# Second layer's down product: high and low weight halves side by side as one moving operand of 512 columns

## The chip, the core and the metric

The kernel runs on one core of one Trainium2 chip. The metric is the device time of one execution, in microseconds (us). Before the change three runs took 3819.11, 3821.22 and 3822.73 us; their median is 3821.22 us.

The engines are named as in the profile: PE is TensorE's matmul, PEld its loading of the stationary operand, DVE is VectorE, ACT is ScalarE, POOL is GpSimd, SP is SyncE. The SBUF holds operands, the PSUM (banks of 512 float32 columns on 128 partitions) takes what PE writes.

## The reference, cut to what matters

Three steps follow each other: a convolution along the sequence by FFT, a layer of eight experts with one expert per row, and a dense layer with a squared ReLU. The change is in the last of them.

```python
def _moe2_ref(x, w_in, w_out):          # x: 24576 x 256
    h = np.maximum(x @ w_in, 0.0)       # w_in: 256 x 2048
    return (h * h @ w_out).astype(np.float32)   # w_out: 2048 x 256

def reference(**kwargs):
    attn_out = _attn_ref(**attn_kwargs)          # irfft(rfft(x) * filt), 8 x 3072 x 256
    x = attn_out.reshape(B * S, D)
    x = _moe_ref(x=x, **moe_kwargs)              # w1: 8 x 256 x 1024, w2: 8 x 1024 x 256
    return _moe2_ref(x=x, **moe2_kwargs)
```

The inputs w_in and w_out come as float64; the kernel's matmuls take float32 operands in the rounded form fp32r, so every factor is split into a high part and a low part, and a product is high by high, plus high by low, plus low by high.

## The kernel before, in words

The kernel runs its stages one behind the other on one core: the FFT stage, the expert layer ("layer 1" below, functions up and down, lines 793 to 831), and the dense layer ("layer 2", functions split_t, up2, split_h and down2, lines 853 to 943). Layer 1 multiplies with moving operands of 512 columns (some tiles 256), layer 2 with 256. While layer 1 runs, DVE decodes the float64 weights of layer 2 into high and low parts (decode_all) that stay in SBUF: `woh` and `wol` are the halves of w_out.

Layer 2 takes the 24576 rows in 48 tiles of 512 rows (index t) and the 2048 hidden columns in 8 units of 256 (index u): 384 steps (t, u). The up product up2 forms four 128 x 256 blocks from seven products (prod, line 879); each is three matmuls of 256 columns, 21 in all. They collect in three PSUM banks: V (pool psH, two buffers), G (psX) and P (psH2). ACT and DVE bring them out: ACT copies s1 (L888), p5 (L890), u2 (L895) and C[2] (L903); DVE adds C[0] (L893), C[3] (L899) and C[1] (L900). DVE squares the ReLU into q (L905), split_h rounds q into hh on ACT (L912) and takes the rest hl on DVE (L914).

The down product down2 multiplies slices of hh and hl (stationary, 128 x 128) with rows of woh and wol (moving, 256 columns): 24 matmuls per step, three for each of eight combinations of row block and hidden half. They add up over the 8 units in two PSUM banks, each with the 256 output columns of two row blocks. Tiles with even t use the banks of pool psY, those with odd t the banks of psY2 (py_tiles). After the last unit ACT copies each bank to SBUF (L933) and POOL scatters each row block to the output with an indirect DMA (L936).

The order on each engine is the order in which the code issues. The loop at lines 1025 to 1041 handles three units at a time, in four parts: in pass n, up2 of unit n, split_h of unit n - 1 (ACT's hh in part 1, DVE's hl in part 2, counting from 0) and down2 of unit n - 2. In each part up2 comes first, then split_h, then the piece of down2. So the last down2 of tile t (u = 7) is issued in the pass in which up2 works on unit u = 1 of tile t + 1. Below this pass is called the closing pass of tile t. In it, as in every pass, part 1 of up2 ends with the second product into V and its copy u2; part 2 has the second product into G, the third into V, and the adds L899 (which reads V) and L900 (which reads G); part 3 starts with the fourth product into the same V.

Of the kernel before, what the change touches and what calls it, by code (L numbers as in the profile page):

```python
# [12 lines left out]
F32 = mybir.dt.float32  # L13
F32R = mybir.dt.float32r
# [3 lines left out]
ALU = mybir.AluOpType  # L18
# [4 lines left out]
B, S, D = 8, 3072, 256  # L23
NT = B * S
E, F1 = 8, 1024
F2 = 2048
# [4 lines left out]
TT = 512  # L31
# [71 lines left out]
def spectral_moe_kernel(ctx: ExitStack, tc: tile.TileContext, x, filt_r, filt_i, w_gate, w_og, w1, w2,  # L103
                        w_in, w_out, c_ma, c_mi, c_mb, c_mb2, c_sg, c_cum, out):
    nc = tc.nc
# [6 lines left out]
    outv = dram_disjoint_views(out, NT // 128)  # L112
# [49 lines left out]
    pl = {"xsm": ctx.enter_context(tc.tile_pool(name="xsm", bufs=2, side="right"))}  # L162
# [455 lines left out]
    w2nd, lpool = [], []  # L618
    dcs = ctx.enter_context(ExitStack())

    def decode(pool, src, parts, val=None):


        v = nc.vector
        raw = pool.tile([128, ND, 2], I32, name="raw")
        nc.sync.dma_start(out=raw, in_=src)
        yield
        H, L = raw[:, :, 1], raw[:, :, 0]
        ea = pool.tile([128, ND], I32, name="ea")
        eb = pool.tile([128, ND], I32, name="eb")  # L630
        v.tensor_scalar(ea, H, 20, 0x7FF, op0=ALU.logical_shift_right, op1=ALU.bitwise_and)
        v.tensor_scalar(eb, ea, 896, 0, op0=ALU.subtract, op1=ALU.max)
        v.tensor_scalar(ea, eb, 255, None, op0=ALU.min)
        v.tensor_scalar(eb, ea, 23, None, op0=ALU.logical_shift_left)
        yield
        v.tensor_scalar(ea, H, -2147483648, None, op0=ALU.bitwise_and)
        v.tensor_tensor(eb, ea, eb, ALU.bitwise_or)
        yield
        v.tensor_scalar(ea, H, 0xFFFFF, 3, op0=ALU.bitwise_and, op1=ALU.logical_shift_left)
        mb_ = pool.tile([128, ND], I32, name="mb_")  # L640
        v.tensor_scalar(mb_, ea, 0x3F800000, None, op0=ALU.bitwise_or)
        P = eb.bitcast(F32)
        a = pool.tile([128, ND], F32, name="a")
        v.tensor_tensor(a, mb_.bitcast(F32), P, ALU.mult)
        yield
        v.tensor_scalar(ea, L, 1, None, op0=ALU.logical_shift_right)
        lf = pool.tile([128, ND], F32, name="lf")
        v.tensor_scalar(lf, ea, 2.0 ** -51, None, op0=ALU.mult)
        v.tensor_tensor(lf, lf, P, ALU.mult)
        yield  # L650
        if val is not None:
            v.tensor_tensor(val, a, lf, ALU.add)
        for at, hi, lo in parts:
            v.tensor_tensor(hi, a[:, at], lf[:, at], ALU.add)
            v.tensor_tensor(a[:, at], a[:, at], hi.bitcast(F32), ALU.subtract)
            v.tensor_tensor(lo, a[:, at], lf[:, at], ALU.add)
        yield

    def decode_all():
        wres = ctx.enter_context(tc.tile_pool(name="wres", bufs=1))  # L660


        wsh, wsl = (wres.tile([128, F2 // 256, 7, 128], F32R, name=n) for n in ("wsh", "wsl"))
        woh, wol = (wres.tile([128, F2 // 128, D], F32R, name=n) for n in ("woh", "wol"))
        w2nd.extend((wsh, wsl, woh, wol))
        lpool.append(ctx.enter_context(tc.tile_pool(name="rp2", bufs=2)))
        pool = dcs.enter_context(tc.tile_pool(name="dcp", bufs=1))
        first, second = slice(0, 128), slice(128, 256)
        for u in range(F2 // 256):
            a0, a1 = (pool.tile([128, ND], F32, name=f"val{c}") for c in range(2))  # L670
            for c, val in enumerate((a0, a1)):
                yield from decode(pool, w_in32[c * 128:(c + 1) * 128, 2 * u * ND:2 * (u + 1) * ND]
                                  .rearrange("p (n two) -> p n two", two=2),
                                  [(at, wsh[:, u, i], wsl[:, u, i])
                                   for at, i in (((first, 0),), ((first, 1), (second, 2)))[c]], val)
            sc = pool.tile([128, 4, 128], F32, name="sc")
            v.tensor_tensor(sc[:, 0], a0[:, second], a1[:, second], ALU.add)
            v.tensor_tensor(sc[:, 1], sc[:, 0], a0[:, first], ALU.subtract)
            v.tensor_tensor(sc[:, 2], a0[:, first], a0[:, second], ALU.subtract)
            v.tensor_tensor(sc[:, 3], a1[:, first], sc[:, 1], ALU.subtract)  # L680
            yield
            nc.scalar.copy(wsh[:, u, 3:7], sc)
            v.tensor_tensor(wsl[:, u, 3:7], sc, wsh[:, u, 3:7].bitcast(F32), ALU.subtract)
            yield
        for f in range(F2 // 128):
            yield from decode(pool, w_out32[f * 128:(f + 1) * 128].rearrange("p (d two) -> p d two", two=2),
                              [(slice(0, D), woh[:, f, :], wol[:, f, :])])


    psm = ctx.enter_context(ExitStack())  # L690
# [18 lines left out]
    def py_tiles(t):  # L709
        return [pl["psY2" if t % 2 and "psY2" in pl else "psY"].tile([128, TT], F32, name=f"py{h}") for h in range(2)]  # L710
# [6 lines left out]
    slot, k = [], 0  # L717
# [120 lines left out]
    NU = F2 // 256  # L838
    R, X2, H2, Z = {}, {}, {}, {}
# [78 lines left out]
    def down2(t, u):  # L918

        hh, hl = H2[t, u]  # L920
        woh, wol = w2nd[2:4]
        if u == 0:
            Z[t] = [p.rearrange("p (c d) -> p c d", c=2) for p in py_tiles(t)]
        for m in range(24):
            k, i, c, n = m // 12, m // 6 % 2, m // 3 % 2, m % 3
            x, w = ((hh, woh), (hl, woh), (hh, wol))[n]
            nc.tensor.matmul(Z[t][k][:, c, :], x[:, 2 * i + k, c * 128:(c + 1) * 128], w[:, 2 * u + i, :],  # L927
                             start=u == 0 and m in (0, 12), stop=u == NU - 1 and m in (11, 23), skip_group_check=True)
            if u == NU - 1 and m in (11, 23):
                if k == 0:  # L930
                    Z[t].append(pl["oup"].tile([128, 4, D], F32, name="ou"))
                ou = Z[t][2]
                nc.scalar.copy(ou[:, 2 * k:2 * k + 2, :], Z[t][k])  # L933
                io = X2[t][2]
                for c in range(2 * k, 2 * k + 2):
                    nc.gpsimd.indirect_dma_start(out=outv[4 * t + c], out_offset=bass.IndirectOffsetOnAxis(ap=io[:, c:c + 1], axis=0),  # L936
                                                 in_=ou[:, c, :], in_offset=None)
            if m in (2, 8, 17):
                yield
        del H2[t, u]  # L940
        if u == NU - 1:
            del X2[t], Z[t]
        yield
# [59 lines left out]
    def steps_m():  # L1003
        for n in range(len(jobs) + LAG1):
            if n < len(jobs):
                t, f = jobs[n]
                up(t, f)
                step_1(t, f)
            if n >= LAG1:
                down(*jobs[n - LAG1])  # L1010
            yield
        for _ in dec[0]:
            pass
        dcs.close()
        used = nc.values_load(usedi[0:1, 0:1], min_val=0, max_val=NTILE_T)
        with tc.If(used > NTILE_T - NX):
            for t in range(NMAIN, NTILE1):
                extra(t)
        m1.close()
        xgs.close()  # L1020
        open_m2()
        st = split_t(0)
        for _ in st:
            pass
        for n in range(len(units2) + 2):
            g = up2(*units2[n]) if n < len(units2) else iter(())
            t, u = units2[min(n, len(units2) - 1)]
            d = down2(*units2[n - 2]) if n >= 2 else iter(())
            for part in range(4):
                next(g, None)  # L1030
                if part == 0 and 0 < n <= len(units2):
                    sh = split_h(*units2[n - 1])
                if part in (1, 2) and n:
                    next(sh, None)
                next(d, None)
            if u == 2 and t + 2 < NTILE2:
                load_t(t + 2)
            if u == 3 and t + 1 < NTILE2:
                st = split_t(t + 1)
            next(st, None)  # L1040
            yield
# [43 lines left out]
    m = steps_m()  # L1085
# [4 lines left out]
    for i, k in enumerate(order):  # L1090
# [3 lines left out]
        n = done["a"]  # L1094
# [24 lines left out]
    tables()  # L1119
    open_left()  # L1120
    dec.append(decode_all())
    for _ in m:
        pass
# [33 lines left out]
```

## Time and profile before

| what | value |
|---|---|
| median of three runs | 3821.22 us |
| profiled execution, its time | 3831.18 us |
| profiled execution, its span (first to last instruction) | 3829.5 us |
| mean granted clock of PE | 0.994 |
| PE busy | 3762.7 us, 98% of the span |
| DVE busy | 2767.0 us, 72% |
| ACT busy | 1973.5 us, 52% |
| POOL busy | 608.2 us, 16% |
| layer 2's matmuls of down2 (L927) | 3 x 3072 |
| layer 2's stretch | from about 1800 us to the end |

The busy time of PE is the sum over pipelined matmuls whose ends are modelled, so a matmul's length in a row (0.28 us for 256 columns) is longer than the step from its start to the next start. The step is what a matmul costs in a dense stream, and it is read from the first column of the timeline.

### The profile page before, as it was taken

What the parts mean: (1) busy time and instruction counts of PE and PEld (TensorE: products, weight loads), DVE (VectorE), ACT (ScalarE), POOL (GpSimd) and SP (SyncE); (2) the same over time, 40 slices, a digit from 0 to 9 for tenths busy, and PEclk for the clock granted to TensorE, in tenths of its full rate; (3) what the DMA queues carried; (4) which work ended last, traced back from release to release, by engine and by line L of the source; (5) the groups of instructions that cost most, each with busy time, mean ns of one, the idle gap of its engine ahead of it and who ended that gap; (6) DMA issues with size and microseconds to landing.
All of it is one profiled execution on the core that took longest, in us unless ns stands there. A gap on an engine that the chain in (4) does not pass through costs nothing.

```text
span 3829.5 us, 73425 instructions
## 1 busy us (share of the span) xinstructions
PE 3762.7 (98%) x27256; PEld 3512.9 (92%) x27256; DVE 2767.0 (72%) x5038; ACT 1973.5 (52%) x3909; POOL 608.2 (16%) x641
## 2 busy tenths in 40 slices
PE   8999999999999999999999999999999999999998
PEld 7888877788888888888999999999999999999998
DVE  6678685688888866655777777777777777777776
ACT  6466463354545545544555555555555555555554
POOL 3477575000000000000001100100110010011001
PEclk9999999999999999999999999999999999999999
DMA  6333322455555545543010010001001000100100
GB/s 194 100 117 113 105 86 91 142 158 165 170 163 173 178 150 161 164 148 114 23 29 23 29 29 23 29 23 29 23 29 29 23 29 23 29 23 29 29 18 18
DMA packets 262750, 309.30 MB, mean 81 GB/s; under 512 B 75153, under 2 KB 206194, under 8 KB 262386
## 3 DMA queue, kind: packets, MB, share of 16 engines
q1 hardware_dynamic: 242928, 252.39, 21.8%
q0 software_dynamic: 18432, 51.93, 3.8%
q8 instruction: 215, 3.52, 0.4%
q14 instruction: 149, 1.22, 0.1%
q10 hardware_dynamic: 1026, 0.23, 0.0%
HBM read 224.01 MB, written 80.45 MB: 80 GB/s over the span
## 4 chain that ended last, share of the span: by engine, by line
PE 37%; issue 14%; POOL 2%; DVE 0%; ACT 0%; POOLq 0%; DVEq 0%; ACTq 0%
PE py L927 20%; PE ph L881 13%; PE px L881 5%; POOL out_dram L936 2%; DVE tc L867 0%; DVE bl L871 0%; DVE hl L914 0%; DVE bl L861 0%; ACT bh L869 0%; POOLq L1152 0%; DVE C L899 0%; ACT ou L933 0%; ACT bh L860 0%; ACT u L895 0%; DVE C L900 0%
## 5 line engine op out<-in xcount | busy, mean ns | idle before, releaser
L927 PE MATMUL py<-woh,hh 128*128 128x256 f32 x3072 | 857.2, 279 | 0.0
L927 PE MATMUL py<-woh,hl 128*128 128x256 f32 x3072 | 852.8, 278 | 0.4 <-DVE hl L914 0.4
L927 PE MATMUL py<-wol,hh 128*128 128x256 f32 x3072 | 852.9, 278 | 0.0
L936 POOL DMA_INDIRECT out_dram<-ou,ix x192 | 214.0, 1115 | 2935.7 <-ACT ou L933 2891.8
L927 PEld LDWEIGHTS py<-woh,hl 128*128 128x128 f32 x3072 | 579.9, 189 | 0.9 <-DVE hl L914 0.8
L927 PEld LDWEIGHTS py<-woh,hh 128*128 128x128 f32 x3072 | 579.9, 189 | 0.0
L927 PEld LDWEIGHTS py<-wol,hh 128*128 128x128 f32 x3072 | 576.3, 188 | 0.0
L806 ACT ACTIVATE hh<-ph 128x512 fp32r<-128x512 f32 (+1 forms) x472 | 251.8, 533 | 586.3 <-PE ph L802 559.3
L881 PE MATMUL ph<-bh,wsh 128*128 128x256 f32 x1920 | 541.5, 282 | 5.6 <-ACT bh L860 4.4
L881 PE MATMUL ph<-bh,wsl 128*128 128x256 f32 x1920 | 539.2, 281 | 0.0
L881 PE MATMUL ph<-bl,wsh 128*128 128x256 f32 x1920 | 539.0, 281 | 0.0
L905 DVE SCALAR_TENSOR_TENSOR q<-C 128x1024 f32<-128x1024 f32 x384 | 468.3, 1220 | 2.3 <-ACT C L903 2.2
L808 DVE SCALAR_TENSOR_TENSOR hl<-ph,hh 128x512 fp32r<-128x512 f32 (+1 forms) x472 | 286.8, 608 | 253.4 <-ACT hh L806 248.5
L914 DVE TENSOR_TENSOR hl<-q,hh 128x1024 fp32r<-128x1024 f32 x384 | 467.1, 1217 | 1.1 <-ACT hh L912 1.1
L899 DVE TENSOR_TENSOR C<-ph,p 128x256 f32<-128x256 f32 x384 | 163.5, 426 | 417.1 <-ACT hh L912 412.8
L903 ACT COPY C<-ph 128x256 f32<-128x256 f32 x384 | 143.0, 372 | 519.7 <-PE ph L881 518.2
L912 ACT CAST hh<-q 128x1024 fp32r<-128x1024 f32 x384 | 403.1, 1050 | 1.3 <-DVE q L905 1.3
L881 PEld LDWEIGHTS ph<-bh,wsh 128*128 128x128 f32 x1920 | 363.0, 189 | 6.9 <-issue 4.6
L881 PEld LDWEIGHTS ph<-bl,wsh 128*128 128x128 f32 x1920 | 361.6, 188 | 0.0
L881 PEld LDWEIGHTS ph<-bh,wsl 128*128 128x128 f32 x1920 | 361.5, 188 | 0.0
L819 PE MATMUL py<-hh,wh 128*128 128x512 f32 (+1 forms) x944 | 348.4, 369 | 0.0
L802 PE MATMUL ph<-xh,wh 128*128 128x512 f32 (+1 forms) x944 | 340.3, 360 | 0.0
(261 smaller groups left out, 8184.2 us busy)
## 6 DMA issues: line engine op xcount, KB each, us to landing
r<-in_moe_w_dram SPq DMA_DIRECT2D x448, 256.0 KB
xt<-in_x_dram SPq DMA_DIRECT2D x48, 512.0 KB
r<-ytd SPq DMA_DIRECT2D x48, 512.0 KB
xg<-srt SPq DMA_DIRECT2D x41, 544.0 KB
ytd<-yt SPq DMA_DIRECT2D x41, 512.0 KB
xg<-srt SPq DMA_DIRECT2D x18, 272.0 KB
ytd<-yt SPq DMA_DIRECT2D x18, 256.0 KB
raw<-in_moe_w_in_dram SPq DMA_DIRECT2D x16, 256.0 KB
```

Of the source, the lines that this page charges most:

```text
L802: nc.tensor.matmul(ps, a[:, c, f2 * 128:(f2 + 1) * 128], b[:, c, 0:w], start=n == 0, stop=n == 5)
L806: nc.scalar.activation(hh, ps, AF.Relu)
L808: nc.vector.scalar_tensor_tensor(hl, ps, 0.0, hh.bitcast(F32), op0=ALU.max, op1=ALU.subtract)
L819: nc.tensor.matmul(Y[t][h], a[:, f % 2, h * 128:(h + 1) * 128], b, start=f == 0 and i == 0, stop=f == NF - 1 and i == 2)
L881: nc.tensor.matmul(ps, x[:, u, a], y[:, b], start=start and n == 0, stop=n == 2, skip_group_check=True)
L899: nc.vector.tensor_tensor(C[:, 3], V, p5, ALU.add)
L903: nc.scalar.copy(C[:, 2], V)
L905: nc.vector.scalar_tensor_tensor(q, C, 0.0, C, op0=ALU.max, op1=ALU.mult)
L912: nc.scalar.copy(hh, q)
L914: nc.vector.tensor_tensor(hl, q, hh.bitcast(F32), ALU.subtract)
L927: nc.tensor.matmul(Z[t][k][:, c, :], x[:, 2 * i + k, c * 128:(c + 1) * 128], w[:, 2 * u + i, :], start=u == 0 and m in (0, 12), stop=u == ...
L936: nc.gpsimd.indirect_dma_start(out=outv[4 * t + c], out_offset=bass.IndirectOffsetOnAxis(ap=io[:, c:c + 1], axis=0), in_=ou[:, c, :], in_o ...
```

## The change

The two halves of w_out are stored side by side in one tile `wo`, so that for each row of 128 hidden values the 256 high columns and the 256 low columns are 512 neighbouring columns. In down2 a slice of hh now multiplies all 512 columns in one matmul, and a slice of hl the 256 high columns. The left half of the bank then collects high by high and low by high, the right half high by low. So a step has 16 matmuls, eight of 512 and eight of 256 columns, where it had 24 of 256. Each row block needs a whole bank: four banks per tile, two of psY and two of psY2, for every t. At the end of a tile, for each of the four row blocks b, ACT copies the left half to SBUF (now 256 columns), DVE adds the right half to it, and POOL's indirect DMA waits for DVE.

```diff
-        woh, wol = (wres.tile([128, F2 // 128, D], F32R, name=n) for n in ("woh", "wol"))
-        w2nd.extend((wsh, wsl, woh, wol))
+        wo = wres.tile([128, F2 // 128, 2, D], F32R, name="wo")
+        w2nd.extend((wsh, wsl, wo))
...
         if u == 0:
-            Z[t] = [p.rearrange("p (c d) -> p c d", c=2) for p in py_tiles(t)]
-        for m in range(24):
-            k, i, c, n = m // 12, m // 6 % 2, m // 3 % 2, m % 3
-            x, w = ((hh, woh), (hl, woh), (hh, wol))[n]
-            nc.tensor.matmul(Z[t][k][:, c, :], x[:, 2 * i + k, c * 128:(c + 1) * 128], w[:, 2 * u + i, :],
-                             start=u == 0 and m in (0, 12), stop=u == NU - 1 and m in (11, 23), skip_group_check=True)
-            if u == NU - 1 and m in (11, 23):
-                if k == 0:
+            Z[t] = [pl[n].tile([128, TT], F32, name=f"py{h}") for n in ("psY", "psY2") for h in range(2)]
+        for m in range(16):
+            b, i, n = m // 8 * 2 + m // 2 % 2, m // 4 % 2, m % 2
+            w = D if n else 2 * D
+            at = 2 * i + b // 2, slice(b % 2 * 128, b % 2 * 128 + 128)
+            nc.tensor.matmul(Z[t][b][:, 0:w], (hl if n else hh)[:, at[0], at[1]],
+                             wo[:, 2 * u + i].rearrange("p s d -> p (s d)")[:, 0:w],
+                             start=u == 0 and i == 0 and n == 0, stop=u == NU - 1 and i == 1, skip_group_check=True)
+            if u == NU - 1 and i == 1 and n == 1:
+                if b == 0:
                     Z[t].append(pl["oup"].tile([128, 4, D], F32, name="ou"))
...
-                nc.scalar.copy(ou[:, 2 * k:2 * k + 2, :], Z[t][k])
...
+                nc.scalar.copy(ou[:, b, :], Z[t][b][:, 0:D])
+                nc.vector.tensor_tensor(ou[:, b, :], Z[t][b][:, D:2 * D], ou[:, b, :], ALU.add)
+                nc.gpsimd.indirect_dma_start(out=outv[4 * t + b], out_offset=bass.IndirectOffsetOnAxis(ap=X2[t][2][:, b:b + 1], axis=0),
+                                             in_=ou[:, b, :], in_offset=None)
-            if m in (2, 8, 17):
+            if m in (1, 5, 11):
                 yield
```

The points at which down2 hands over to up2 keep the same share of columns in each part: 3, 6, 9 and 6 matmuls of 256 columns before, 2, 4, 6 and 4 matmuls (half of them of 512) now.

DVE's order in the closing pass of one tile, before: the adds of up2, hl, the square q, and then the next pass.

```order
L893 TENSOR_TENSOR C<-ph,s_27598 128x256
L899 TENSOR_TENSOR C<-ph,p_27599 128x256
L900 TENSOR_TENSOR C<-px,u_27600 128x256
L914 TENSOR_TENSOR hl_27622<-q,hh_27621 128x1024
L905 SCALAR_TENSOR_TENSOR q<-C 128x1024
```

The same pass on DVE now (L936 is the new add of a bank's right half; each new name of py is one of the four banks):

```order
L893 TENSOR_TENSOR C<-ph,s_26983 128x256
L936 TENSOR_TENSOR ou<-py_26573,ou 128x256
L899 TENSOR_TENSOR C<-ph,p_26984 128x256
L900 TENSOR_TENSOR C<-px,u_26985 128x256
L914 TENSOR_TENSOR hl_27006<-q,hh_27005 128x1024
L936 TENSOR_TENSOR ou<-py_26574,ou 128x256
L905 SCALAR_TENSOR_TENSOR q<-C 128x1024
L936 TENSOR_TENSOR ou<-py_26575,ou 128x256
L936 TENSOR_TENSOR ou<-py_26576,ou 128x256
```

Four adds are new; the first stands between L893 and L899, the second between hl and q, the other two behind q.

ACT's order in the closing pass now (before, one L933 of 512 columns stood behind L912 and one behind L903):

```order
L888 COPY s_26983<-ph 128x256
L890 COPY p_26984<-px 128x256
L895 COPY u_26985<-ph 128x256
L912 CAST hh_27005<-q 128x1024
L935 COPY ou<-py_26573 128x256
L935 COPY ou<-py_26574 128x256
L903 COPY C<-ph 128x256
L935 COPY ou<-py_26575 128x256
L935 COPY ou<-py_26576 128x256
```

The copy of the first bank stands directly behind the rounding of hh; DVE's first add reads what this copy writes.

## Rows read from the trace of the kernel before

**Rows 1.** The page: the span, and PE's line of busy time.

```profile
span 3829.5 us, 73425 instructions
PE 3762.7 (98%) x27256; PEld 3512.9 (92%) x27256; DVE 2767.0 (72%) x5038; ACT 1973.5 (52%) x3909; POOL 608.2 (16%) x641
```

**Rows 2.** Busy time by stretch: layer 2's. Columns: window, length, then engines in us.

```profile
core 0: us, PE busy (x) PEld busy (x) DVE busy (x) ACT busy (x) POOL busy (x), PEclk, DMA share, GB/s
1850.00:3790.00 1940.00, 1940.00 (x16678) 1939.69 (x16676) 1429.86 (x2222) 1009.66 (x2132) 210.21 (x188) 1.00 0.09 26
```

**Rows 3.** Timeline of PE, layer 2, one pass. Columns: start, length, engine, line, operation.

```profile
2524.76 0.28 PE L881 MATMUL ph<-bh,wsh 128*128 128x256 f32 x1
...
2525.79 0.28 PE L881 MATMUL ph<-bh,wsh 128*128 128x256 f32 x1
...
2527.21 0.28 PE L881 MATMUL px<-bh,wsh 128*128 128x256 f32 x1
...
2527.56 0.28 PE L881 MATMUL ph<-bh,wsh 128*128 128x256 f32 x1
...
2528.93 0.28 PE L881 MATMUL ph<-bh,wsh 128*128 128x256 f32 x1
...
2529.99 0.28 PE L881 MATMUL ph<-bh,wsh 128*128 128x256 f32 x1
```

**Rows 4.** Timeline of PE in layer 1, where 512 and 256 columns mix.

```profile
1201.01 0.39 PE L802 MATMUL ph<-xh,wh 128*128 128x512 f32 x1
...
1203.05 0.28 PE L802 MATMUL ph<-xh,wh 128*128 128x256 f32 x1
1203.16 0.28 PE L802 MATMUL ph<-xl,wh 128*128 128x256 f32 x1
...
1203.76 0.40 PE L819 MATMUL py<-hh,wh 128*128 128x512 f32 x1
...
1205.15 0.28 PE L802 MATMUL ph<-xh,wh 128*128 128x256 f32 x1
...
1207.60 0.28 PE L802 MATMUL ph<-xh,wh 128*128 128x256 f32 x1
...
1210.00 0.28 PE L819 MATMUL py<-hh,wl 128*128 128x256 f32 x1
```

**Rows 5.** Timeline of ACT in one closing pass.

```profile
2521.53 0.37 ACT L895 COPY u<-ph 128x256 f32<-128x256 f32 x1 [0.68 <-PE ph L881]
2521.79 1.05 ACT L912 CAST hh<-q 128x1024 fp32r<-128x1024 f32 x1
```

**Rows 6.** Timeline of DVE in the same closing pass.

```profile
2521.18 0.42 DVE L893 TENSOR_TENSOR C<-ph,s 128x256 f32<-128x256 f32 x1 [0.45 <-PE ph L881]
2522.94 0.43 DVE L899 TENSOR_TENSOR C<-ph,p 128x256 f32<-128x256 f32 x1 [1.33 <-ACT hh L912]
2523.28 0.41 DVE L900 TENSOR_TENSOR C<-px,u 128x256 f32<-128x256 f32 x1
2523.61 1.22 DVE L914 TENSOR_TENSOR hl<-q,hh 128x1024 fp32r<-128x1024 f32 x1
```

**Rows 7.** Timeline of PE in the same closing pass: the end of part 1, the start of part 3.

```profile
2521.86 0.28 PE L927 MATMUL py<-wol,hh 128*128 128x256 f32 x1
...
2523.69 0.28 PE L881 MATMUL ph<-bh,wsh 128*128 128x256 f32 x1
```

**Rows 8.** Timeline of layer 2's first passes: ACT, DVE and PE, each waiting for another.

```profile
1799.88 1.04 ACT L869 CAST bh<-tc 128x1024 fp32r<-128x1024 f32 x1 [2.02 <-DVE tc L867]
...
1800.95 1.23 DVE L871 TENSOR_TENSOR bl<-tc,bh 128x1024 fp32r<-128x1024 f32 x1 [1.11 <-ACT bh L869]
...
1811.13 0.42 DVE L899 TENSOR_TENSOR C<-ph,p 128x256 f32<-128x256 f32 x1 [1.31 <-PE ph L881]
...
1811.61 0.39 PE L881 MATMUL ph<-bh,wsh 128*128 128x256 f32 x1 [0.59 <-DVE C L899]
...
1811.84 0.28 PE L881 MATMUL ph<-bl,wsh 128*128 128x256 f32 x1
```

More of the change, by code (lines that the diff above doesn't have):

```diff
@@ L686, in decode_all @@
             yield from decode(pool, w_out32[f * 128:(f + 1) * 128].rearrange("p (d two) -> p d two", two=2),
-                              [(slice(0, D), woh[:, f, :], wol[:, f, :])])
+                              [(slice(0, D), wo[:, f, 0], wo[:, f, 1])])
     psm = ctx.enter_context(ExitStack())
@@ L920, in down2 @@
         hh, hl = H2[t, u]
-        woh, wol = w2nd[2:4]
+        wo = w2nd[2]
         if u == 0:
-            Z[t] = [p.rearrange("p (c d) -> p c d", c=2) for p in py_tiles(t)]
-        for m in range(24):
-            k, i, c, n = m // 12, m // 6 % 2, m // 3 % 2, m % 3
-            x, w = ((hh, woh), (hl, woh), (hh, wol))[n]
-            nc.tensor.matmul(Z[t][k][:, c, :], x[:, 2 * i + k, c * 128:(c + 1) * 128], w[:, 2 * u + i, :],
-                             start=u == 0 and m in (0, 12), stop=u == NU - 1 and m in (11, 23), skip_group_check=True)
-            if u == NU - 1 and m in (11, 23):
-                if k == 0:
-                    Z[t].append(pl["oup"].tile([128, 4, D], F32, name="ou"))
-                ou = Z[t][2]
-                nc.scalar.copy(ou[:, 2 * k:2 * k + 2, :], Z[t][k])
[L934 to L937, printed above, removed]
-            if m in (2, 8, 17):
+            Z[t] = [pl[n].tile([128, TT], F32, name=f"py{h}") for n in ("psY", "psY2") for h in range(2)]
[8 more added lines that the diff above has]
+                if b == 0:
+                    Z[t].append(pl["oup"].tile([128, 4, D], F32, name="ou"))
+                ou = Z[t][4]
+                nc.scalar.copy(ou[:, b, :], Z[t][b][:, 0:D])
[3 more added lines that the diff above has]
+            if m in (1, 5, 11):
                 yield
```

## The prediction

> **What bounds the kernel now.** I read the page's head first: PE is busy 98% of the span [rows 1], so the question is only whether PE's stream gets shorter or gets new holes. Then the busy times by stretch: in the 1940 us of layer 2 between 1850 and 3790 us PE is never idle, at a granted clock of 1.00 (the 2.4 GHz level), DVE is busy 1429.86 us (74%) and ACT 1009.66 us (52%) [rows 2]. 16678 matmuls of 256 columns in 1940 us are 116.3 ns from start to start. DVE and ACT have time to spare on average; what counts is whether one of their instructions that PE waits for comes later than PE does. For that I read the timeline.
>
> **What a matmul of layer 2 costs.** One pass, from the first product into V to the next, takes 2529.99 - 2524.76 = 5.23 us for 45 matmuls [rows 3], 116.2 ns each. Within it the step is not even: 12 matmuls from 2527.56 to 2528.93 take 114.2 ns each, 12 from 2525.79 to 2527.21 take 118.3 ns [rows 3]. In layer 1, 9 matmuls of 512 columns from 1201.01 to 1203.05 take 226.7 ns each [rows 4]: twice 113.3, so a column costs the same there as in layer 2's quick stretches, and a wide matmul as such saves little. Where layer 1 alternates six matmuls of 256 and six of 512, the wide ones take (1205.15 - 1203.76)/6 = 231.7 ns and the narrow ones (1203.76 - 1203.05)/6 = 118.3 ns, but the first narrow one behind a wide one takes 0.11 us (1203.05 to 1203.16) [rows 4].
>
> **Removed: eight matmuls and eight weight loads per step.** Three matmuls of 256 columns become one of 512 and one of 256: the columns, 768, stay the same, and what can go is only the part of a matmul's cost that doesn't grow with its columns. Before, three cost 3 x 116.2 = 348.6 ns. The pair is not in the trace of before in this order. Lower end: 226.7 + 114.2 = 340.9 ns, a gain of 7.7 ns. Upper end: 231.7 + 118.3 = 350.0 ns, a loss of 1.4 ns. The nearest rows are those of the mixed stretch, since the new stream mixes too, and in it every narrow matmul stands right behind a wide one: 231.7 + 114.2 = 345.9 ns, a gain of 2.7 ns. There are 8 x 384 = 3072 such threes: -8.3 us, with ends -23.7 and +4.3 us. All of it is on the path, as PE has no idle time here.
>
> **Added: four adds on DVE and two more copies on ACT per tile.** By busy time this is nothing: an add like L893 takes 0.42 us [rows 6], four of them 1.7 us in a tile of 8 x 5.23 = 41.8 us, in which DVE has 26% idle. But the first add stands in DVE's queue between L893 and L899, and it waits for ACT's copy, which stands behind the rounding of hh. Followed through the closing pass in the trace:
>
> - PE finishes the first bank's last matmul at the end of part 1, about 2521.86 + 0.28 = 2522.14 [rows 7]; the columns of part 1 are unchanged.
> - ACT starts hh at 2521.79 for 1.05 us, to 2522.84 [rows 5]. The copy behind it is long released. Neighbours on ACT overlap by 0.11 us (L895 ends at 2521.90, L912 starts at 2521.79 [rows 5]), so the copy starts at 2522.73 and, as 256 columns like L895, takes 0.37 us: 2523.10.
> - DVE has been idle since 2521.60 and waits. An instruction released by ACT starts 0.03 us after ACT's end (1799.88 + 1.04 = 1800.92, then 1800.95 [rows 8]): the add starts at 2523.13.
> - L899 follows it at the distance that L900 has from L899, 0.34 us [rows 6]: at 2523.47 instead of 2522.94, ending at 2523.90 instead of 2523.37.
> - Part 3's first matmul writes the V bank that L899 reads and must wait for it. Layer 2's second pass shows this wait and its price: L899 ends at 1811.13 + 0.42 = 1811.55, the matmul starts at 1811.61, and the next one 0.23 us later, 0.11 us more than the usual step [rows 8]. So here: start at 2523.96 instead of 2523.69 [rows 7], and 0.11 us more behind it: 0.38 us.
>
> Tiles 0 to 46 have such a pass (the last tile's closing pass has no up2): 47 x 0.38 = +17.9 us. Bounds: if the copy could start when the bank is ready, the add would be done before L899 was due, and the price is 0; if each hand-over takes 0.1 us more than in the rows (two of them), 0.58 us, 27.3 us.
>
> Does PE win it back? No: it is the engine without slack, and the three-unit pipeline only moves on. Is something else late next? With all times moved as above, hl starts at 2523.47 + 0.67 = 2524.14 [rows 6] and ends at 2525.36; its first use is the eighth matmul of the next pass, before seven steps of 116.2 ns after 2524.76 [rows 3], at 2525.57, now 0.38 us later, so it is in time by 0.6 us. The second add ends near 2525.7, q near 2526.8, the last two adds near 2527.5. The next pass's L899 was due near 2528.2 and is due 0.4 us later now, so the delay ends there.
>
> **Four banks for every tile instead of two in turn.** The next tile's first down2 writes the same four banks in the next pass. The first bank is free at 2523.5 and written after 2525.4; the last is free near 2527.5 and written in part 2 of the next pass, where layer 2's part 2 starts at 2527.21 [rows 3] and six matmuls of up2 and four of down2 stand before it, so after 2528.6. Over a microsecond is left: no cost. The decode of w_out writes the same number of elements with the same instructions, under layer 1: no cost.
>
> **Sum.** -8.3 + 17.9 = +9.6 us on the profiled execution's 3831.18 us. That execution is 10 us (0.26%) above the median of the three runs, most of layer 2 being the same work in both, so I add the difference to the median: 3821.2 + 9.6 = 3831 us, 0.25% slower. Measurement of this kernel tells about 0.2%, 7.6 us, from no change.
>
> **Rivals.**
>
> (a) Instructions bind, not columns. In layer 1's run of narrow matmuls each takes exactly (1210.00 - 1207.60)/20 = 120.0 ns [rows 4], 6 ns more than in the quick stretches, as if each load and matmul cost a fixed time to hand out. If layer 2's 116.2 ns are a mix of such a bound and of columns at 113.3 ns per 256, then a pass with 37 instead of 45 pairs is bound by columns alone, up2's 21 matmuls too: 45 x (116.2 - 113.3) = 130 ns less per pass, x 384 = -50 us; with the wait above -32 us, 3789 us. For it: the even 120.0. Against it: six wide matmuls behind such a run still cost 231.7 rather than 226.7 ns each, though their pairs have time to be handed out, and layer 2 has quick stretches of twelve narrow ones. By half of it the time is 3821 - 25 + 18 = 3814 us.
>
> The Trainium skill, page "TensorE: Matmul & The Clock Gate", section "Wait — 56ns, not 53.3ns?", says that where hardware decoding is off the sequencer spends about 62 ns on each matmul and becomes the bound once a matmul's work in the array is shorter. The run at 120.0 ns for a load and a matmul fits twice 60; layer 2's 114.2 ns does not. By that rule 37 pairs would take 37 x 120 = 4.44 us, below the 5.1 us of columns, which is rival (a) at its full size.
>
> (b) The wait doesn't show, because the gain in part 0 to 2 or a quicker copy lets L899 come in time: -8.3 us alone, 3813 us. For it: PE's slack to L899 is only missed by 0.3 us. Against it: hh's rounding is 1.05 us long and stands ahead of the copy in the order.
>
> (c) The wait is dearer, or spreads: the adds two to four push q and the next L893 far enough that the next pass waits as well, at the same place and price: 2 x 17.9 - 8.3 = +27.5 us, 3849 us. It decides if DVE's chain in the closing pass is 0.7 us longer than I made it.
>
> **Chances.** Forecast 0.58; (a) 0.18, of which 0.06 at its full size; (b) 0.14; (c) 0.10. The forecast's own range, from its bounds for the pair (-23.7 to +4.3) and for the wait (around 17.9), is 3820 to 3843 us, most of it above 3828. Cutting off (a) at full size and the upper part of (c), the range for 8 in 10 is 3806 to 3843 us. Slower by over 0.2%: 0.39 of the forecast and (c), 0.49. Within 0.2%: 0.19 of the forecast, 0.05 of (a), 0.07 of (b), 0.31. Faster: 0.13 of (a), 0.07 of (b), 0.20.
>
> **What will show it.** In the timeline after: a closing pass in which L936 comes at about 2523.1 on the old scale, L899 directly behind it, and part 3's first matmul 0.39 us long with DVE's L899 named as what released it, 47 times, and PE free of waits in all other passes. A usual pass of 37 matmuls of 5.21 us (8 x 2.7 ns less than 5.23) bears out the gain; 5.10 us would be rival (a). The forecast is wrong if part 3 starts without a wait, if a usual pass is under 5.16 us, or if PE waits for the adds at the start of a tile.

## The result, and the profile after

The changed kernel took 3841.27 us, median of 5 runs (3839.03 to 3843.92), against 3821.22 us before (five runs by then, the same median as of the first three): 20.05 us more, a ratio of 1.0052 with a 95% interval of 1.004 to 1.0064. The forecast was 3831 us and slower; the time lies inside its range of 3806 to 3843 us, near the upper end.

The page after: the span, PE's share, and the two groups of down2's matmuls (operation, count, then busy time and mean ns of one).

```profile
span 3842.2 us, 67659 instructions
PE 3779.6 (98%) x24184; PEld 3387.8 (88%) x24184; DVE 2828.6 (74%) x5230; ACT 1990.1 (52%) x4005; POOL 616.6 (16%) x641
L928 PE MATMUL py<-wo,hh 128*128 128x512 f32 x3072 | 1142.2, 394 | 0.0
L928 PE MATMUL py<-wo,hl 128*128 128x256 f32 x3072 | 866.0, 282 | 0.4 <-DVE hl L914 0.4
```

PE has 3072 matmuls and loads fewer than in [rows 1] and is busy 17 us longer. So the change did what it says to the number of instructions, and the time did not fall with them.

Layer 2 of the kernel after by stretch, in the columns of [rows 2].

```profile
1850.00:3790.00 1940.00, 1936.77 (x13552) 1800.73 (x13552) 1473.12 (x2380) 1011.74 (x2196) 209.00 (x180) 1.00 0.09 25
```

The granted clock of this stretch is still 1.00, so no part of the loss in it is the clock's. A pass now has 37 matmuls, so 13552 are 366.3 passes of 5.297 us on average; 16678/45 passes of before were 5.235 us [rows 2]. 62 ns more in each of 384 passes is 23.8 us. It comes in two portions, which the timeline separates.

**A usual pass.** PE of the kernel after, part 1 and the following pass's start (start, length, engine, line, operation).

```profile
2511.27 0.29 PE L881 MATMUL ph<-bh,wsh 128*128 128x256 f32 x1
...
2513.02 0.39 PE L928 MATMUL py<-wo,hh 128*128 128x512 f32 x1
2513.25 0.28 PE L928 MATMUL py<-wo,hl 128*128 128x256 f32 x1
2513.36 0.40 PE L928 MATMUL py<-wo,hh 128*128 128x512 f32 x1
2513.60 0.28 PE L928 MATMUL py<-wo,hl 128*128 128x256 f32 x1
2513.72 0.29 PE L881 MATMUL px<-bh,wsh 128*128 128x256 f32 x1
...
2516.53 0.29 PE L881 MATMUL ph<-bh,wsh 128*128 128x256 f32 x1
```

Read starts, since lengths overlap. Two pairs take 2513.72 - 2513.02 = 0.70 us, 350 ns each, where the prediction has 348.6 ns for three narrow matmuls. The pass takes 2516.53 - 2511.27 = 5.26 us. Over all usual passes of the two traces (all but the closing ones) the medians are 5.253 us after and 5.233 us before, the means 5.2552 and 5.2367 us. 0.0185 to 0.020 us more in 384 passes: +7.1 to +7.7 us, where -8.3 us had been forecast. All of it lies in down2: by the means a pair takes 350.2 ns where three narrow matmuls of down2 took 347.9 ns, 2.3 ns more 3072 times, and a matmul of up2 takes 116.8 ns in both.

**A closing pass.** DVE, ACT and PE of the kernel after; this one lies about 2.7 us earlier on the scale than the one of [rows 5 to 7].

```profile
2518.20 0.42 DVE L893 TENSOR_TENSOR C<-ph,s 128x256 f32<-128x256 f32 x1 [0.48 <-PE ph L881]
2520.15 0.42 DVE L936 TENSOR_TENSOR ou<-py,ou 128x256 f32<-128x256 f32 x1 [1.53 <-ACT ou L935]
2520.50 0.41 DVE L899 TENSOR_TENSOR C<-ph,p 128x256 f32<-128x256 f32 x1
2520.83 0.41 DVE L900 TENSOR_TENSOR C<-px,u 128x256 f32<-128x256 f32 x1
2521.16 1.21 DVE L914 TENSOR_TENSOR hl<-q,hh 128x1024 fp32r<-128x1024 f32 x1
```

```profile
2518.53 0.37 ACT L895 COPY u<-ph 128x256 f32<-128x256 f32 x1 [0.67 <-PE ph L881]
2518.80 1.05 ACT L912 CAST hh<-q 128x1024 fp32r<-128x1024 f32 x1
2519.75 0.85 ACT L935 COPY ou<-py 128x256 f32<-128x256 f32 x2
```

```profile
2518.85 0.29 PE L928 MATMUL py<-wo,hl 128*128 128x256 f32 x1
...
2520.62 0.28 PE L928 MATMUL py<-wo,hl 128*128 128x256 f32 x1
2520.96 0.39 PE L881 MATMUL ph<-bh,wsh 128*128 128x256 f32 x1
2521.19 0.28 PE L881 MATMUL ph<-bl,wsh 128*128 128x256 f32 x1
```

DVE stands 1.53 us idle before L936, for ACT's copy, which stands behind hh. L899 has no bracket, since L936 stands right ahead of it: the delay is to be seen one instruction earlier. L899 starts 2.30 us after L893, against 1.76 us in [rows 6]. PE's step from the last narrow matmul of part 2 to part 3 is 2520.96 - 2520.62 = 0.34 us instead of 0.12, and the next is 0.23 us instead of 0.12. Both together are 0.33 us. Over the 47 closing passes the median is 5.596 us against 5.253 us of the others, the mean 5.602 against 5.255: 0.34 to 0.35 us. Times 47: +15.6 us by the rows, +16.3 us by the means.

The waits of the kernel after between 1850 and 3800 us name the releaser (engine and line, what it waited for: us in total, times, longest).

```profile
PEld ph L881 <- DVE C L899: 18.9, 49, 0.7
...
DVE ou L936 <- ACT ou L935: 70.6, 46, 1.8
```

7.1 and 15.6 are 22.7 us, 7.1 and 16.3 are 23.4 us. From layer 2's first matmul to the end of the span it is 3842.2 - 1787.38 = 2054.8 us after and 3829.5 - 1797.89 = 2031.6 us before: +23.2 us. The two starts, of before and of after:

```profile
1797.89 0.55 PE L881 MATMUL ph<-bh,wsh 128*128 128x256 f32 x1 [4.39 <-ACT bh L860]
```

```profile
1787.38 0.55 PE L881 MATMUL ph<-bh,wsh 128*128 128x256 f32 x1 [4.26 <-ACT bh L860]
```

The profiled spans themselves differ by only 12.7 us, because the profiled execution of before spent 10.5 us more ahead of layer 2. Its own time was also 10 us above its median. What it waited for there I have not followed; so layer 2 is compared by itself.

### The profile page after: what moved, and what is told of

Read it like the earlier page. It is cut to its first block, busy times and chain, and to the rows that moved or that the text cites. A ratio compares the mean times of both kernels' runs of the same rounds, so it can differ in the third digit from the quotient of the medians.

```text
span 3842.2 us, 67659 instructions
## 1 busy us (share of the span) xinstructions
PE 3779.6 (98%) x24184; PEld 3387.8 (88%) x24184; DVE 2828.6 (74%) x5230; ACT 1990.1 (52%) x4005; POOL 616.6 (16%) x641
## 4 chain that ended last, share of the span: by engine, by line
PE 49%; ACT 2%; issue 1%; DVE 1%; POOL 0%; ACTq 0%; POOLq 0%; DVEq 0%
PE py L928 25%; PE ph L881 17%; PE px L881 7%; ACT hh L912 1%; DVE ou L936 1%; DVE C L899 0%; ACT ou L935 0%; ACT u L895 0%; POOL out_dram L937 0%; ACTq L935 0%; DVE tc L867 0%; POOLq L1153 0%; DVE bl L871 0%; DVE bl L861 0%; ACT bh L869 0%
## 5 line engine op out<-in xcount | busy, mean ns | idle before, releaser
L928 PE MATMUL py<-wo,hh 128*128 128x512 f32 x3072 | 1142.2, 394 | 0.0
L928 PE MATMUL py<-wo,hl 128*128 128x256 f32 x3072 | 866.0, 282 | 0.4 <-DVE hl L914 0.4
L937 POOL DMA_INDIRECT out_dram<-ou,ix x192 | 222.0, 1156 | 2951.1 <-DVE ou L936 2920.6
L928 PEld LDWEIGHTS py<-wo,hh 128*128 128x128 f32 x3072 | 578.0, 188 | 61.1
L928 PEld LDWEIGHTS py<-wo,hl 128*128 128x128 f32 x3072 | 577.0, 188 | 0.9 <-DVE hl L914 0.9
L903 ACT COPY C<-ph 128x256 f32<-128x256 f32 x384 | 143.1, 373 | 553.3 <-PE ph L881 553.3
L912 ACT CAST hh<-q 128x1024 fp32r<-128x1024 f32 x384 | 404.0, 1052 | 1.3 <-DVE q L905 1.3
L899 DVE TENSOR_TENSOR C<-ph,p 128x256 f32<-128x256 f32 x384 | 162.6, 423 | 328.7 <-ACT hh L912 262.6
L819 PE MATMUL py<-hh,wh 128*128 128x512 f32 (+1 forms) x944 | 348.6, 369 | 0.0
L802 PE MATMUL ph<-xl,wh 128*128 128x512 f32 (+1 forms) x944 | 338.4, 358 | 0.7 <-DVE xl L787 0.7
L819 PE MATMUL py<-hl,wh 128*128 128x512 f32 (+1 forms) x944 | 338.4, 358 | 0.0
```

Of the source, the lines that this page charges most:

```text
L802: nc.tensor.matmul(ps, a[:, c, f2 * 128:(f2 + 1) * 128], b[:, c, 0:w], start=n == 0, stop=n == 5)
L819: nc.tensor.matmul(Y[t][h], a[:, f % 2, h * 128:(h + 1) * 128], b, start=f == 0 and i == 0, stop=f == NF - 1 and i == 2)
L899: nc.vector.tensor_tensor(C[:, 3], V, p5, ALU.add)
L903: nc.scalar.copy(C[:, 2], V)
L912: nc.scalar.copy(hh, q)
L928: nc.tensor.matmul(Z[t][b][:, 0:w], (hl if n else hh)[:, at[0], at[1]], wo[:, 2 * u + i].rearrange("p s d -> p (s d)")[:, 0:w], start=u == ...
```

## The experiments

Two questions: whether the hand-over copy, add, L899, part 3 makes the 15.6 us, and what makes a pair dearer than three narrow matmuls. Times are medians, with the ratio to the kernel before on the same chip; the ratio is an estimate over all runs and not always the quotient of the two medians (e8: 1.0061, the medians give 1.0051). "Pass" is the mean between 1850 and 3770 us: 1920 us divided by the number of passes, which is the count of PE's matmuls in the row of the stretch divided by 37 (45 where all are narrow). For e7 it is the stretch from 1850 to 3580 us and 29 matmuls. For the kernel after it is 5.297 us there too:

```profile
1850.00:3770.00 1920.00, 1916.77 (x13411) 1781.98 (x13411) 1458.40 (x2359) 1002.07 (x2177) 209.00 (x180) 1.00 0.09 26
```

| kernel | median us | ratio [95%] | before there | pass us |
|---|---|---|---|---|
| e1 late add | 3824.50 | 1.0012 [1.0003, 1.0021] | 3819.33 | 5.254 |
| e4 copy first | 3824.38 | 1.0013 [1.0004, 1.0022] | 3819.33 | 5.254 |
| e2 grouped | 3818.78 | 1.0 [0.9991, 1.0009] | 3819.33 | 5.240 |
| e3 narrow, four banks | 3818.22 | 0.9996 [0.9987, 1.0005] | 3819.33 | 5.236 |
| e8 before with an add | 3852.36 | 1.0061 [1.0044, 1.0078] | 3832.73 | 5.291 |
| e5 six changes | 3827.64 | 0.9987 [0.9977, 0.9996] | 3832.73 | 5.224 |
| e6 equal 384 | 3831.32 | 1.0 [0.9991, 1.001] | 3832.73 | 5.240 |
| e7 wide only | 3599.47 | 0.9396 [0.938, 0.9411] | 3832.73 | 4.63 |
| e9 square last | 3807.87 | 0.9965 [0.9953, 0.9977] | 3822.49 | 5.210 |
| e10 low last | 3815.92 | 0.9983 [0.9974, 0.9992] | 3822.49 | 5.229 |

**The wait, taken away (e1).** The two banks that were closed at the ends of parts 1 and 2 are both closed at the end of part 2, the others at the end of down2. So no copy and add stand ahead of L899.

```diff
-            if u == NU - 1 and i == 1 and n == 1:
...
+            if u == NU - 1 and m in (11, 15):
+                for c in (0, 1) if m == 11 else (2, 3):
+                    close(c)
```

close(b) holds the allocation, copy, add and DMA of one bank, unchanged; the kernels below that call it do so in the same way.

> The changed kernel, but the first two banks of a closing tile are copied and added at the end of part 2 (behind hl on DVE, behind hh on ACT), the last two at the end of part 3. Theory: the closing pass loses 0.33 us because L899 stands behind the first add; with the add behind L899 all passes take 5.25 us and the time falls by 47 x 0.33 = 15.6 us, to about 3826 us. Rival (four banks or more evictions cost the time in another way): within 4 us of 3841.

The waits of PE for L899 between 1850 and 3770 us, of the kernel after and of e1:

```profile
PEld ph L881 <- DVE C L899: 18.5, 48, 0.7
```

```profile
PEld ph L881 <- DVE C L899: 0.2, 1, 0.2
```

One wait is left of 48, and the pass is 5.254 us. The loss, each time against before on the same chip, went from 20.05 to 5.2 us: the wait is worth about 15 us, as 47 x 0.33 says.

**The wait, taken away by order alone (e4).** The adds stay where they are; only in part 1 down2's piece is emitted ahead of hh's rounding, so that the copy precedes hh on ACT.

```diff
+                if part == 1:
+                    next(d, None)
...
-                next(d, None)
+                if part != 1:
+                    next(d, None)
```

> The changed kernel, but in part 1 the piece of down2 is issued ahead of split_h, so that on ACT the copy of the first bank stands ahead of the rounding of hh; DVE's order is as in the changed kernel, the first add still ahead of L899. Theory (the add is late only because its copy waits for 1.05 us of rounding): the add is done before L899 is due, no wait of PE in part 3, time falls by 15.6 us to about 3826. Rival (any DVE instruction between L893 and L899 delays PE): less than a third of that, 3836 or more.

A closing pass of e4 on ACT and on DVE:

```profile
2509.64 0.38 ACT L935 COPY ou<-py 128x256 f32<-128x256 f32 x1 [0.27 <-PE py L928]
2509.91 1.05 ACT L912 CAST hh<-q 128x1024 fp32r<-128x1024 f32 x1
```

```profile
2510.05 0.42 DVE L936 TENSOR_TENSOR ou<-py,ou 128x256 f32<-128x256 f32 x1 [0.95 <-ACT ou L935]
2510.39 0.42 DVE L899 TENSOR_TENSOR C<-ph,p 128x256 f32<-128x256 f32 x1
```

The add still stands right ahead of L899, but it is no longer late. PE's weight loads wait for L899 three times in the stretch, 0.6 us in all. Time and pass are those of e1. So it is not the add ahead of L899 that costs but that its copy stands behind hh.

**The wait, put into the kernel before (e8).** Its closing pass gets a copy that nobody needs behind hh and an add of two SBUF tiles behind it, ahead of L899. All else is the kernel before, two banks and narrow matmuls.

```diff
+            if u == NU - 1 and m == 8:
+                ou = pl["oup"].tile([128, 4, D], F32, name="ou")
+                Z[t].append(ou)
+                nc.scalar.copy(ou[:, 0, :], hh[:, 0, :].bitcast(F32))
+                nc.vector.tensor_tensor(ou[:, 1, :], ou[:, 0, :], ou[:, 0, :], ALU.add)
```

> The kernel before (narrow matmuls, two banks in turn), with one needless pair in each closing pass: ACT copies 256 columns behind the rounding of hh, DVE adds what was copied to itself, between L893 and L899. Theory (the wait of part 3 is made by the place of the add alone, whatever the matmuls' width): 47 x 0.33 = +15.6 us on the kernel before, about 3835, and 47 closing passes of about 5.56 us. Rival (the wait needs the four banks or the wide matmuls): less than +5 us.

Its DVE, its PE, and PE's waits:

```profile
2527.60 0.42 DVE L933 TENSOR_TENSOR ou<-ou 128x256 f32<-128x256 f32 x1 [1.57 <-ACT ou L932]
2527.94 0.42 DVE L899 TENSOR_TENSOR C<-ph,p 128x256 f32<-128x256 f32 x1
```

```profile
2528.00 0.28 PE L927 MATMUL py<-wol,hh 128*128 128x256 f32 x1
2528.41 0.38 PE L881 MATMUL ph<-bh,wsh 128*128 128x256 f32 x1
2528.63 0.29 PE L881 MATMUL ph<-bl,wsh 128*128 128x256 f32 x1
```

```profile
PEld ph L881 <- DVE C L899: 15.0, 46, 0.3
```

The step to part 3 is 0.41 us instead of 0.12, the one behind it 0.22: 0.39 us more, 47 times 18.3 us; timed +19.6 us. The same wait with the same releaser arises without a wide matmul in layer 2. It is about 0.05 us longer than in the kernel after, and by the medians of the 47 closing passes L899 starts 2.338 us behind L893 instead of 2.294.

**The pair (e3).** e1's closing, and each wide matmul as two narrow ones of the same stationary operand, into the same four banks.

```diff
-            w = D if n else 2 * D
...
+            for s in (0,) if n else (0, 1):
+                nc.tensor.matmul(Z[t][b][:, s * D:(s + 1) * D], (hl if n else hh)[:, at[0], at[1]], wo[:, 2 * u + i, s],
```

> As the late add, with four banks per tile and high and low halves side by side in the bank, but each wide matmul as two of 256 columns (24 narrow matmuls per step, as before the change). Theory (the pair is dearer than three narrow ones, by (5253 - 5233)/8 = 2.4 ns): a usual pass of 5.233 us, the time 7 us under the late add alone, within 4 us of the kernel before. Rival (the four banks, not the widths, make the pass longer): as the late add alone or above.

e3, and e1 beside it, by stretch:

```profile
1850.00:3770.00 1920.00, 1920.00 (x16501) 1919.76 (x16500) 1474.68 (x2384) 1011.97 (x2201) 242.69 (x181) 1.00 0.09 26
```

```profile
1850.00:3770.00 1920.00, 1920.00 (x13521) 1797.38 (x13520) 1470.28 (x2377) 1008.71 (x2190) 234.87 (x180) 1.00 0.09 26
```

Eight matmuls and loads more in each pass, and 18 ns less: 16501/45 passes against 13521/37. Timed, e3 is 6.3 us faster than e1 and no different from before. That answers two questions: four banks, four copies and four adds cost nothing that these runs can tell (ratio 0.9987 to 1.0005) once they are off the way of L899, and in this order the wide matmul itself is the loss.

**Is it the change of width? (e2, e6)** The idea was that a step costs some 1.6 ns more wherever the width changes, 16 times in a pass. e2 groups each part's wide matmuls ahead of its narrow ones: 8 changes. e6 gives all 16 matmuls 384 columns, 6144 in all as before: 8 changes, against up2's narrow ones.

```diff
+        parts = ((0, 0),), ((1, 0), (0, 1)), ((1, 1), (2, 0), (3, 0)), ((2, 1), (3, 1))
+        for m, (b, i, n) in enumerate((b, i, n) for part in parts for n in range(2) for b, i in part):
```

```diff
-            w = D if n else 2 * D
+            w = D + 128
```

> As the late add, and in each part the wide matmuls stand first and the narrow ones behind them, so that widths change 8 times per pass and not 16. Theory (a change between 512 and 256 columns costs some ns): a usual pass falls from 5.253 to about 5.235 us, 7 us less than the late add alone. Rival (the step depends on the number of matmuls and columns, not on their order): within 2 us of the late add alone.

> As the late add, but all 16 matmuls of a step have 384 columns (high half and half of the low half), as many columns in all. It leaves out the right part of high by low and adds a left part of low by low; the add on DVE has 128 columns. Theory (changes of width cost): 8 changes per pass and smaller ones, a usual pass of 5.240 us or less. Rival (sixteen matmuls wider than 256 are dearer by themselves, with or without changes): 5.250 or more.

```profile
1850.00:3770.00 1920.00, 1920.00 (x13557) 1797.21 (x13556) 1473.77 (x2382) 1010.30 (x2201) 223.94 (x181) 1.00 0.08 26
```

```profile
1850.00:3770.00 1920.00, 1920.00 (x13556) 1919.67 (x13556) 1447.41 (x2383) 1015.45 (x2201) 264.78 (x184) 1.00 0.09 26
```

The first is e2, the second e6. Both come to 5.240 us, 13 ns less than e1: 8 x 1.6. Taken alone the two bear the idea out.

**The idea fails (e5, e9, e10).** Three orders with 6 changes each. e5 spreads down2 over the parts as 1 wide and 1 narrow; 3 wide; 4 wide and 1 narrow; 6 narrow. It closes bank 0 at the end of part 2 and the others at the end of down2:

```diff
+        order = ((0, 0, 0), (0, 0, 1),
+                 (0, 1, 0), (1, 0, 0), (1, 1, 0),
+                 (2, 0, 0), (2, 1, 0), (3, 0, 0), (3, 1, 0), (0, 1, 1),
+                 (1, 0, 1), (1, 1, 1), (2, 0, 1), (2, 1, 1), (3, 0, 1), (3, 1, 1))
```

> As the late add, but the wide matmuls stand together in the first three parts (1, 3 and 4 of them, with one narrow one at the end of the first and of the third) and part 3 has six narrow ones: 6 changes of width per pass, the parts as long as before. The first bank is closed at the end of part 2, the others at the end of part 3. Theory (each change of width costs about (5253.5 - 5240.5)/8 = 1.6 ns): a usual pass of 5.237 us, 3 ns under the grouped order's 5.2405. Rival (only wide against narrow right behind each other in one bank cost): 5.240 or more.

Its usual pass takes 5.207 us by the median, where 6 changes should give some 5.237. But its mean is 5.224:

```profile
1850.00:3770.00 1920.00, 1920.00 (x13598) 1792.86 (x13597) 1476.37 (x2389) 1008.23 (x2206) 214.56 (x184) 1.00 0.09 26
```

The difference looks like an order on DVE again. Three banks close at the end of down2, and their adds stand behind q:

```profile
2519.47 0.42 DVE L929 TENSOR_TENSOR ou<-py,ou 128x256 f32<-128x256 f32 x1
2519.80 1.22 DVE L905 SCALAR_TENSOR_TENSOR q<-C 128x1024 f32<-128x1024 f32 x1
2520.94 1.08 DVE L929 TENSOR_TENSOR ou<-py,ou 128x256 f32<-128x256 f32 x3
```

PE's matmuls and loads in the pass that follows:

```profile
2521.20 0.99 PE L940 MATMUL py<-wo,hh 128*128 128x512 f32 x3
2521.47 0.30 PEld L940 LDWEIGHTS py<-wo,hh 128*128 128x128 f32 x2 [0.18 <-PE ph L881]
2522.04 0.28 PE L881 MATMUL px<-bh,wsh 128*128 128x256 f32 x1
```

In the next pass the group of three wide matmuls that starts at 2521.20 takes 0.84 us to the next start instead of 0.69, in 47 passes some 7 us. Its second matmul writes the bank that the first of these adds frees at 2520.94 + 0.41 = 2521.35, and its load starts only at 2521.47. The profile names PE itself as the releaser there, so that the add is the cause is a reading; e9 tests it. It is e5 with q emitted at the end of every pass, in a closing pass behind the adds:

```diff
+        yield
         q = pl["cp"].tile([128, 4, 256], F32, name="q")
...
+            next(g, None)
```

> As the six changes, and the square q is issued at the very end of each pass, so that in a closing pass DVE's adds of the banks stand ahead of q. The six changes had a usual pass of 5.207 us and lost 0.147 us in 49 of the closings, where the next pass's wide matmuls waited for the second bank. Theory (they waited because q's 1.22 us stood ahead of that bank's add): no such wait, all passes 5.207 us, 7 us under the six changes, 0.27% under the kernel before. Rival (the banks are late for another reason, or q is late now and hh after it): as the six changes or slower.

```profile
1850.00:3770.00 1920.00, 1920.00 (x13635) 1798.94 (x13634) 1477.96 (x2395) 1013.85 (x2207) 207.23 (x184) 1.00 0.09 26
```

5.210 us over all passes, 5.207 by the median: with the adds ahead of q the waits are gone, and the time is 14.6 us below that of before on the same chip, 0.9965 [0.9953, 0.9977]. From layer 2's first matmul to the end the traces have 10.6 us of it (2021.0 us against 2031.6); where the other 4 us lie is not shown. This version is faster than the kernel before and, by the two ratios, than the kernel after. e10 is e9 with the low part's eight narrow matmuls last (2 wide; 3 wide; 3 wide and 2 narrow; 6 narrow):

```diff
+        order = ((0, 0, 0), (0, 1, 0),
+                 (1, 0, 0), (1, 1, 0), (2, 0, 0),
+                 (2, 1, 0), (3, 0, 0), (3, 1, 0), (0, 0, 1), (0, 1, 1),
+                 (1, 0, 1), (1, 1, 1), (2, 0, 1), (2, 1, 1), (3, 0, 1), (3, 1, 1))
```

> As the run with q last, but with the narrow matmuls all in the last two parts (2 wide; 3 wide; 3 wide and 2 narrow; 6 narrow), also 6 changes of width. Theory (narrow matmuls in a long run behind wide ones take 113.3 ns, a single narrow one between wide ones 119 or more): usual pass of 5.200 us or less. Rival (the order within down2 matters little beyond the six narrow ones at the end): 5.207 us. A third outcome would be a pass over 5.22 us: then the step's extra nanoseconds don't follow from the order of widths.

PE in part 3, e9 first, then e10: the six narrow matmuls as one row, and the next pass's start.

```profile
2509.21 0.84 PE L941 MATMUL py<-wo,hl 128*128 128x256 f32 x6
2509.89 0.28 PE L881 MATMUL ph<-bh,wsh 128*128 128x256 f32 x1
```

```profile
2509.36 0.87 PE L941 MATMUL py<-wo,hl 128*128 128x256 f32 x6
2510.07 0.28 PE L881 MATMUL ph<-bh,wsh 128*128 128x256 f32 x1
```

The same six instructions, in the same place behind the same three of up2, take 113.3 ns each in e9 and 118.3 in e10. Both orders have 6 changes, and their passes are 19 ns apart. So the number of changes alone doesn't set the cost; it happened to fall together with it in e2 and e6. Nor is a step's excess tied to what runs beside it on the other engines: in a linear fit over the traces of ten of these kernels (2000 to 3700 us) the time that each kind of instruction on DVE, ACT and POOL spends beside a step accounts for under a tenth of the steps' variance. The orders also differ in which banks and which stationary slices follow each other, and no run separates that. What sets the few ns stays open.

**Wide alone (e7).** e1 without the narrow matmuls, to read the cost of the wide ones by themselves.

```diff
+            if n:
...
+                continue
```

> As the late add, with the eight narrow matmuls of hl left out (low by high isn't computed). Theory (a pass is the sum of its steps, 8 changes): the grouped order's 5.2405 us less 8 x 118.7 ns = 4.29 us a pass, about 3819 - 365 = 3454 us. Rival (handing out instructions was a bound, and with 29 pairs it no longer is): columns alone, 9472 x 0.443 ns = 4.19 us a pass, about 3416 us.

The largest of its PE waits between 1850 and 3580 us:

```profile
PEld ph L881 <- DVE C L899: 125.5, 350, 0.7
```

A miss: the theory had 4.29 us and the rival 4.19, and 10837 matmuls, 29 to a pass, are 373.7 passes of 4.63 us in 1730 us. PE now waits for L899 in nearly every pass, 0.36 us each. The run says nothing on widths, but it shows something else: with 8 x 118.7 ns = 0.95 us of matmuls out of the pass, over a third of it comes back as waits, most of them for the same L899 as in the closing passes.

## Why the prediction came out right in sign and low in size

The forecast was +9.6 us on the median, the measurement +20.05 us. One of its two terms was right, the other had the wrong sign; the sign of the sum came out because the term that was right is the larger one.

- **Removed matmuls: the failed term.** The step that failed is the choice of 345.9 ns for a pair inside bounds of 340.9 and 350.0. It took the quick stretch's 114.2 ns [rows 3] for the narrow matmul, on the strength of one step of 0.11 us read off two starts rounded to 0.01 us in layer 1 [rows 4]. The mixed stretch's mean, 118.3 ns, was the upper bound. Measured in the kernel after, as medians: 230.9 ns for the wide matmul (231.7 was right) and 119.1 ns for the narrow one. The pair takes 350.0 ns by these, 350.2 by the means: the upper bound. The three that it replaced were off too: 348.6 ns is the mean of all 45 matmuls of a pass, and down2's own took 347.9 ns. So the gain of 8.3 us became a loss of 7.1 us, outside the ends given for this term (-23.7 and +4.3 us); e3 against e1 shows the sign directly. The pass of 5.21 us that was to bear out the gain did not come, it took 5.253. What the step took for granted, that a cost per matmul goes when the matmul goes, did not hold in this order; in e9's order the pair takes 344.7 ns and the gain is there.
- **The added wait: right.** Its place, releaser, count and chain came out as written: L936 right ahead of L899, part 3's first matmul with a length of 0.39 us, DVE's L899 named. 0.33 to 0.35 us instead of 0.38, 15.6 to 16.3 us instead of 17.9; e1 and e4 take it away, e8 makes it elsewhere.
- **The sum.** With the measured terms it is 22.7 to 23.4 us, which has the 23.2 us of the two traces between its ends and is about 3 us above the timed 20.05; one profiled execution of each doesn't tell whether that rest is more than scatter.
- **Four banks, two more copies, four adds: nothing that shows.** e3 has them all, off the way of L899, and runs as before does.
- **Rival (a), instructions bind.** Wrong: a usual pass is 5.253 us, not 5.10. And six loads and matmuls at 113.3 ns each, in e9, leave no room for 120 ns for handing out a pair.
- **Rival (b), the wait doesn't show; (c), it spreads.** Neither: 47 closing passes are longer, and the passes behind them are usual ones.

The Trainium skill, page "TensorE: Matmul & The Clock Gate", section "Wait — 56ns, not 53.3ns?", gives each matmul a fixed cost of about 2.5 ns beside its columns, once the array is at full clock. By that, as an estimate, eight matmuls fewer shorten a pass by 20 ns. The trace disagrees here: from e3 to e1 eight fewer lengthen it by 18 ns, and e9 has the gain, 24 to 26 ns below before, with the very same matmuls as e1 in another order.

## What to carry to other kernels

However short an instruction is that is put into an engine's queue, what stands behind it waits as long as it does, and where the busiest engine needs that, the wait is paid there. So look at which long instruction its source stands behind (hh here), and if one is there, emit the source ahead of it or the new instruction later, as e4 and e1 do. When a stream that is busy all the time is to lose instructions at the same columns, take the cost of the new mix from a stretch's mean and not from one step, and let the forecast be no gain until a run shows one. Then try a few orders, since between the worst and the best order of the same 37 matmuls here lie 44 ns in a pass, 17 us.

## What the runs showed of the hardware that was not expected

- At a granted clock of 1.00 the same matmul of 256 columns has a step of 113.3 ns in one place of the stream and 118 in another, with no wait that the profile shows; the passes repeat it (e9's start at 2504.68, 2509.89 and 2515.10 us, 5.21 us apart each time). The six matmuls of part 3 have it both ways in e9 and e10 behind the same three of up2, so it depends on more than the matmul and what stands right ahead of it.
- Columns alone, at 113.3 ns for 256, would make a pass 45 x 113.3 = 5.10 us. No order with all the columns came below a median of 5.207.
- A PE that waited here lost 0.1 us more than the wait: behind part 3's late start the next step is 0.23 us (after) or 0.22 us (e8) instead of 0.12, as in [rows 8].
